# An order of the first units rewritten: a slice of weights fetched later, scores inside the preceding y, k scaled on GpSimd, the first product in two widths

## The chip, the cores and the metric

The kernel runs on one core of one Trainium2 chip. The metric is the device time of one execution in microseconds. All times below come from the profile of one execution of the kernel before, from its trace, or from the three timed runs.

## What is computed

Two stages follow each other. The first is a recurrent retention over 4 batches, 8 heads, 768 steps and a head size of 64; its output, turned to 3072 rows of 512, goes through a gated layer with the weights w_in (512 x 2048) and w_out (2048 x 512):

```python
for t in range(S):
    state = gamma[None, :, None, None] * state + np.einsum('bhd,bhe->bhde', k[:, :, t], v[:, :, t])
    y[:, :, t] = scale * np.einsum('bhd,bhde->bhe', q[:, :, t], state)
...
h = x @ w_in
g = h * (1.0 / (1.0 + np.exp(-h)))
return (g @ w_out)
```

The inputs q, k and v are float32, the weights are float64.

## The kernel before

**Units and products.** The sequence is cut into 6 chunks of 128 steps; a chunk of one batch is a unit, numbered chunk by chunk, so that units 0 to 3 are the four batches of chunk 0. When the four units of a chunk have been through the first stage, their output x (512 rows of 512) is multiplied by 16 slices of w_in, each of 128 columns. "Product (c, f)" is chunk c by slice f. The products are kept, after the gate, in DRAM (`g_dram`), and the second half of the kernel multiplies them by w_out. For accuracy x and the weights are each split in three parts, and a product is 12 matmuls of 512 columns: 8 into `ha`, 4 into `hb`.

**Steps of a unit.** `T(n)` (`stage_t`) transposes k and q on TensorE (L476, from unit 10 on in halves, L485), and ScalarE copies the results out (L477). `K(n)` (`scale_k`, L418) scales k in place. `SC(n)` makes the sums over k and v (`stage_s`, L504) and the scores (`stage_a`, L514). `A(n)` is called three times: the decay mask on VectorE (L522), the middle state (L528 on ScalarE in chunk 0, L530 on VectorE later) and the next state (L534). `Q(n)` (L423) scales q. `YA(n)` and `YB(n)` are the two halves of the unit's output y on TensorE (`stage_y`, L562); between them stands a fence, a one-element memset on GpSimd (L406) that waits for the first half. `X(n)`, called in turn, copies y out (L609) and splits it in three: L633 on ScalarE, then `lower` (L636) and `third` (L639) on VectorE. `KA(n)` scales k on ScalarE (L909).

**Weights.** `load_w(i)` fetches slice i with three transfers (one at L186 and two at L188, 512 KB in all) into one of two staging buffers. `W(i)`, called step by step, turns float64 into float32 (L205 and L212 on ScalarE, L208, L214, L218 and L224 on VectorE) and splits it (L121, L124, L127, L129). `CL(f)` takes a product out: a copy from `ha` on ScalarE (L744), the subtraction of `hb` on VectorE (L749), the gate on ScalarE (L754); `put_g` stores it (L760).

**Order.** The instructions of the first part, up to the line `early_order.close()`, stand on every engine in the order in which the code writes them. `T(10)`, the first step behind that part, meets q of unit 10. TensorE's instructions stand in written order all through. `fill` and `narrow` are matmuls of zeros that are put in where TensorE would pause; their numbers stand in tables (`FILL_T`, `FILL_Y` and so on), by unit. The transposed k and the two accumulators of a product take turns in three PSUM banks (`turn`), so that every third use meets the same bank.

**Transfers.** All go through SP's queue, in its order: k, q and v of unit 0, the first slice of w_in, units 1 to 3, the second slice, units 4 and 5, the third slice, units 6 and 7, the first stored product, and so on:

```python
for n in range(EARLY - 2):
    for name in "kqv":
        load(name, n)
    if n in (0, 3):
        load_w(n // 3)
```

`EARLY` is 8 and `FAR` is 14. q from unit 8 on has two buffers, k and v three.

Of the kernel before, what the change touches and what calls it, by code (L numbers as in the profile page):

```python
# [34 lines left out]
def kernel(  # L35
# [28 lines left out]
    nc = tc.nc  # L64
# [248 lines left out]
    def fill(out, n, start=True):  # L313

        cols = out.shape[-1] // 128
        for _ in range(n):
            nc.tensor.matmul(out, lhsT=zero, rhs=zero.unsqueeze(1).to_broadcast([128, cols, 128]),
                             start=start, stop=True, skip_group_check=True)

    def narrow(out, n):  # L320

        for _ in range(n):
            nc.tensor.matmul(out[:, :32], lhsT=zero, rhs=zero[:, :32], start=True, stop=True,
                             skip_group_check=True)

    for n in range(EARLY - 2):
        for name in "kqv":
            load(name, n)
        if n in (0, 3):
            load_w(n // 3)  # L330


    ident = const.tile([128, 128], FP32, tag="ident", name="ident")
# [58 lines left out]
    def banks(tag, name, n=2):  # L392
        return ps_u.tile([128, n, 512], FP32, tag=tag, name=name)
# [17 lines left out]
    def scale_k(n):  # L411
        if 0 <= n < len(units):
            t = kqv["k"][n]
            if units[n][0] == NC - 1:
                t = t[:D]
            g = gk[: t.shape[0], units[n][0], :].unsqueeze(2).to_broadcast([t.shape[0], H, D])
            engine = nc.gpsimd if 2 * B + 1 < n < FAR else nc.vector
            engine.tensor_tensor(out=t, in0=t, in1=g, op=ALU.mult)  # L418

    def scale_q(n):  # L420
# [29 lines left out]
        nc.scalar.copy(out=to[n].bitcast(U16).rearrange("p a (t w) -> p w a t", w=2),  # L450
                       in_=turned.pop((name, n)).rearrange("p (w a) t -> p w a t", w=2))

    FILL_T = {2: (3, 2), 3: (0, 1)}
    NARROW_T = {0: (8, 5)}
    FILL_Y = {0: 1, 3: 4}
    NARROW_Y = {0: 8}
    idle = []
    FILL_FENCE = {0: 2, 2: 2, 3: 2}
    FILL_P = {(0, 0): 1, (1, 0): 2}

    def stage_t(n):

# [28 lines left out]

    def score_tile(n):
        u = banks("s", f"sc_{n}")
        sc, sums = (u[:, :, ts(i, 4 * D)].rearrange("p o (a t) -> p o a t", a=HP)
                    for i in range(2))
        return sc, sums
# [46 lines left out]
    def stage_y(n):  # L543

        vs, amn, qtn = kqv["v"].pop(n), am.pop(n), qt.pop(n)
        states = steps_of.pop(n)
        bank = banks("y", f"y_{n}")
        fill(bank[:, 0], FILL_Y.get(n, 0))
        narrow(bank[:, 0], NARROW_Y.get(n, 0))
        yp = bank[:, :, : 4 * D].rearrange("p o (a t) -> p o a t", a=HP)  # L550
        lone = None
        if n == len(units) - 1:
            lone = banks("s", f"yl_{n}")[:, :, : 4 * D].rearrange("p o (a t) -> p o a t", a=HP)

        started, done, new = set(), [], []

        def product(a, o, j, lhsT, rhs, apart_now=False):
            e = j ^ (a % 2)
            to = lone if apart_now else yp
            o = o ^ 1 if apart_now else o  # L560
            key = apart_now, e, o
            i = nc.tensor.matmul(to[ts(e, D), o, a, :], lhsT=lhsT, rhs=rhs,  # L562
                                 start=key not in started, stop=True,
                                 skip_group_check=True).ins
            started.add(key)
            if new:
                fence(done[-1], i)
                new.clear()
            done.append(i)

        def scores():
            for a in range(HP):
                for o in range(2):
                    for j in range(2):
                        product(a, o, j, vs[ts(o, D), 2 * a + j, :], amn[ts(o, D), j, a, :])

        def states_with(part):

            if lone is None:
                new.extend([part] * part)  # L580
            for a in range(HP):
                for o in range(2):
                    j = o ^ part
                    if states[o] is not None:
                        product(a, o, j, states[o][ts(j, D), a, :], qtn[ts(j, D), a, ts(o, D)],
                                part == 1 and lone is not None)
            if part == 0:
                fill(bank[:, 0, 4 * D :], FILL_FENCE.get(n, 0), False)

        if lone is not None:  # L590
            alone[:] = [lone]
        return scores, states_with, yp
# [6 lines left out]
    def steps_y(n, yp):  # L599
        c, b = units[n]  # L600
        if b == 0:
            p, tag = (wpool, "wq") if c == LATE else (xpool, "xt")
            xt[c] = p.tile([128, 3, KIN, NT], FP32R, tag=tag, name=f"xt_{c}")
        raw = None
        if c < LATE:
            if n == 0:
                raws.append(wpool.tile([128, LATE * B, KIN, C], FP32, tag="wq", name="ys"))
            raw = raws[0][:, n]
            nc.scalar.copy(out=raw.rearrange("p a (o t) -> p o a t", o=2), in_=yp)  # L609
        elif c == LATE:  # L610
            raw = hpool.tile([128, KIN, C], FP32, tag="hs", name=f"ys_{n}")
            nc.scalar.copy(out=raw.rearrange("p a (o t) -> p o a t", o=2), in_=yp)
            nc.sync.dma_start(out=y_dram[b], in_=raw)
        elif alone:
            raw = hpool.tile([128, KIN, C], FP32, tag="hs", name=f"ys_{n}")
            to = raw.rearrange("p a (o t) -> p o a t", o=2)
            nc.scalar.copy(out=to, in_=yp)
            for o in range(2):
                for e in range(2):
                    x, z = (t[ts(e, D), i, e ^ o ^ 1 :: 2, :]  # L620
                            for t, i in ((to, o), (alone[0], 1 - o)))
                    nc.vector.tensor_tensor(out=x, in0=x, in1=z, op=ALU.add)
        yield from split_x(c, b, yp, raw)

    def split_x(c, b, y, raw):
        yield
        x = [xt[c][:, i, :, ts(b, C)] for i in range(3)]
        if raw is None:
            src = y
            xh, xl = (t.rearrange("p a (o t) -> p o a t", o=2) for t in x[:2])  # L630
        else:
            (xh, xl), src = x[:2], raw
        held[:] = [nc.scalar.activation(out=xh, in_=src, func=AF.Copy, scale=HALF).ins]  # L633

        def lower():
            nc.vector.tensor_tensor(out=xl, in0=src, in1=xh.bitcast(FP32), op=ALU.subtract)  # L636

        def third():
            nc.vector.scalar_tensor_tensor(out=x[2], in0=x[1].bitcast(FP32),  # L639
                                           scalar=-1.0 / EPS, in1=x[0].bitcast(FP32),  # L640
                                           op0=ALU.mult, op1=ALU.add)

        def rest():
            lower()
            third()

        if c > LATE or c == LATE and y is not None:
            behind_next.append(rest)
            return
        yield  # L650
        lower()
        yield
        third()
# [75 lines left out]
    def multiply(c, f):  # L729
        ha, hb = turn(f"ha_{c}_{f}"), turn(f"hb_{c}_{f}")  # L730
        fill(ha, FILL_P.get((c, f), 0))
        for i in range(3):
            for kk in range(KIN):
                nc.tensor.matmul(hb if i == 2 else ha, lhsT=w_sb[f][:, i, ts(kk, 128)],  # L734
                                 rhs=xt[c][:, i, kk, :], start=kk == 0 and i != 1,
                                 stop=kk == KIN - 1 and i != 0)
        return ha, hb

    def close_in(*of):
        list(close_steps(*of))  # L740
# [91 lines left out]
    def YA(n):  # L832
        ys[n] = stage_y(n)
        ys[n][0]()
        ys[n][1](0)

    def YB(n):
        ys[n][1](1)
        ysteps[n] = steps_y(n, ys[n][2])

    def X(n):
        next(ysteps[n], None)
# [3 lines left out]
    def W(i, times=1):  # L846
        if i not in slices:
            slices[i] = early_slice(i)
        for _ in range(times):
            next(slices[i], None)  # L850
# [11 lines left out]
    T(0), K(0)  # L862
    nc.scalar.activation(out=token, in_=lgc[:1, :1], func=AF.Silu)
    SC(0), A(0), Q(0), A(0), A(0)
    W(0), W(0), W(0), W(0), W(0)
    YA(0), YB(0), X(0)
    T(1), K(1)
    W(0)
    load_w(2)
    W(0)  # L870
    X(0), X(0)
    SC(1), A(1)
    W(0)
    A(1)
    Q(1), A(1)
    T(2), K(2)
    W(0), X(0)
    W(0), W(0)
    YA(1), SC(2)
    A(2)  # L880
    YB(1), X(1)
    A(2), Q(2), A(2)
    X(1)
    T(3), K(3)
    X(1), X(1)
    YA(2), YB(2), X(2)
    SC(3), A(3), A(3), Q(3), A(3)
    X(2), W(1), W(1)
    X(2), X(2)
    YA(3), YB(3), X(3), X(3)  # L890
    W(1), W(1)
    T(4)
    X(3), X(3)
    K(4)
    W(1), W(1)
    loads(EARLY - 2), loads(EARLY - 1)
    closing = {}

# [10 lines left out]
            nc.scalar.activation(out=t[:, h, :], in_=t[:, h, :], func=AF.Copy,  # L909
                                 scale=gk[:, units[n][0], h : h + 1])  # L910

    P(0)
    next_chunk()
    SC(4)
    CL(0), CL(0), CL(0)
# [239 lines left out]
```

## Time and profile before

| What | us |
|---|---|
| median of three runs | 613.96 |
| the three runs | 614.32, 613.96, 612.52 |
| profiled execution | 614.34 |
| its span, first to last instruction | 612.6 |
| TensorE matmul busy | 600.9 (98%) |
| VectorE busy | 397.1 (65%) |
| ScalarE busy | 324.5 (53%) |
| GpSimd busy | 32.9 (5%) |

PE is TensorE's matmul row, PEld its weight loads, DVE VectorE, ACT ScalarE, POOL GpSimd, SPq the queue of SyncE that issues the transfers. A busy TensorE isn't TensorE at its peak, since matmuls overlap. The granted clock of TensorE is 1.00 over the span. "Slices" on the page are 40 equal parts of the span, 15.3 us each, and each digit is a share in tenths.

### The profile page before, as it was taken

What the parts mean: (1) busy time and instruction counts of PE and PEld (TensorE: products, weight loads), DVE (VectorE), ACT (ScalarE), POOL (GpSimd) and SP (SyncE); (2) the same over time, 40 slices, a digit from 0 to 9 for tenths busy, and PEclk for the clock granted to TensorE, in tenths of its full rate; (3) what the DMA queues carried; (4) which work ended last, traced back from release to release, by engine and by line L of the source; (5) the groups of instructions that cost most, each with busy time, mean ns of one, the idle gap of its engine ahead of it and who ended that gap; (6) DMA issues with size and microseconds to landing.
All of it is one profiled execution on the core that took longest, in us unless ns stands there. A gap on an engine that the chain in (4) does not pass through costs nothing.

```text
span 612.6 us, 13713 instructions
## 1 busy us (share of the span) xinstructions
PE 600.9 (98%) x5509; PEld 495.9 (81%) x5509; DVE 397.1 (65%) x672; ACT 324.5 (53%) x598; POOL 32.9 (5%) x89
## 2 busy tenths in 40 slices
PE   8898999999999999999999999999999999999997
PEld 6686788888888888888888888888888888888886
DVE  4797898678886676766689774635545463645631
ACT  7688678678676667676698632212221322313211
POOL 3000020100021111210000000000000000000000
PEclk9999999999999999999999999999999999999999
DMA  9999976586799699998777542623524433433301
GB/s 195 209 199 231 258 214 203 160 254 188 258 231 233 154 263 263 258 291 255 248 249 267 169 138 69 206 69 106 169 72 136 137 110 97 152 123 99 107 1 69
DMA packets 144336, 108.90 MB, mean 178 GB/s; under 512 B 101137, under 2 KB 109585, under 8 KB 144273
## 3 DMA queue, kind: packets, MB, share of 16 engines
q1 hardware_dynamic: 144272, 108.03, 62.3%
q8 instruction: 43, 0.70, 0.5%
q14 instruction: 21, 0.16, 0.1%
HBM read 66.06 MB, written 36.70 MB: 168 GB/s over the span
## 4 chain that ended last, share of the span: by engine, by line
PE 92%; DMA 3%; SPq 2%; DVE 2%; issue 1%; ACT 0%; DVEq 0%
PE ha L734 28%; PE o L1088 21%; PE oa L1088 14%; PE hb L734 14%; PE ob L1088 7%; PE y L562 3%; DMA qf<-in_q_dram 2%; PE sc L504 1%; SPq L166 1%; PE sc L514 1%; DMA kqv<-in_v_dram 1%; SPq L188 1%; PE o L1102 0%; PE oa L1102 0%; PE kp L485 0%
## 5 line engine op out<-in xcount | busy, mean ns | idle before, releaser
L734 PE MATMUL ha<-xt,wi 128*128 128x512 f32 x768 | 193.0, 393 | 0.0
L734 PEld LDWEIGHTS ha<-xt,wi 128*128 128x128 f32 x768 | 142.4, 188 | 30.5 <-DVE xt L636 0.2
L1088 PE MATMUL o<-wo,gs 128*128 128x512 f32 x564 | 143.1, 389 | 0.0
L805 ACT ACTIVATE gs<-gr 128x512 fp32r<-128x512 f32 x96 | 53.2, 621 | 139.0 <-issue 138.0
L1088 PEld LDWEIGHTS o<-wo,gs 128*128 128x128 f32 x564 | 105.9, 188 | 22.0
L807 DVE TENSOR_TENSOR gs<-gr,gs 128x512 fp32r<-128x512 f32 x96 | 62.1, 684 | 94.2 <-ACT gs L805 94.2
L1088 PE MATMUL oa<-wo,gs 128*128 128x512 f32 x376 | 115.7, 389 | 0.0
L749 DVE TENSOR_TENSOR g<-g,hb 128x512 f32<-128x512 f32 x96 | 65.7, 684 | 57.6 <-ACT g L744 42.6
L734 PE MATMUL hb<-xt,wi 128*128 128x512 f32 x384 | 102.7, 389 | 0.0
L734 PEld LDWEIGHTS hb<-xt,wi 128*128 128x128 f32 x384 | 72.1, 188 | 15.1
L1088 PEld LDWEIGHTS oa<-wo,gs 128*128 128x128 f32 x376 | 70.5, 188 | 14.6
L754 ACT ACTIVATE g<-g 128x512 f32<-128x512 f32 x96 | 60.3, 629 | 37.7 <-DVE g L749 37.6
L1088 PE MATMUL ob<-wo,gs 128*128 128x512 f32 x188 | 73.1, 389 | 0.0
L744 ACT ACTIVATE g<-ha 128x512 f32<-128x512 f32 x96 | 56.7, 591 | 28.6 <-PE ha L734 19.8
L808 DVE SCALAR_TENSOR_TENSOR gs<-gs 128x512 fp32r<-128x512 f32 x96 | 62.0, 683 | 0.1
L1088 PEld LDWEIGHTS ob<-wo,gs 128*128 128x128 f32 x188 | 35.3, 188 | 7.4
L205 ACT ACTIVATE ca<-wf 128x512 f32<-128x512 f32 x32 | 21.6, 675 | 6.6 <-DVE cs L218 4.0
L522 DVE TENSOR_TENSOR am<-sc,decay 128x512 f32<-128x512 f32 x24 | 16.5, 687 | 11.4 <-PE sc L514 11.4
L1112 ACT ACTIVATE o<-o 128x512 f32<-128x512 f32 x10 | 6.0, 598 | 33.4 <-PE o L1088 33.0
L218 DVE SCALAR_TENSOR_TENSOR cs<-ca,cs 128x512 uint32<-128x512 uint32 x32 | 22.7, 710 | 0.9
L639 DVE SCALAR_TENSOR_TENSOR xt<-xt 128x512 fp32r<-128x512 f32 x28 | 19.9, 715 | 0.7
L562 PE MATMUL y<-qt,mid 64*64 64x64 f32 x376 | 19.4, 220 | 0.4 <-issue 0.4
(122 smaller groups left out, 562.2 us busy)
## 6 DMA issues: line engine op xcount, KB each, us to landing
gd<-g SPq DMA_DIRECT2D x96, 256.0 KB, 3.7
gr<-gd SPq DMA_DIRECT2D x96, 256.0 KB, 2.7
wf<-in_moe_w_out_dram SPq DMA_DIRECT2D x16, 512.0 KB, 4.7
out_dram<-o SPq DMA_DIRECT2D x23, 256.0 KB, 2.1
wf<-in_moe_w_in_dram SPq DMA_DIRECT2D x16, 256.0 KB, 4.6
wf<-in_moe_w_in_dram SPq DMA_DIRECT2D x32, 128.0 KB, 4.1
kf<-in_k_dram SPq DMA_DIRECT2D x16, 256.0 KB, 4.1
qf<-in_q_dram SPq DMA_DIRECT2D x16, 256.0 KB, 4.1
```

The source lines that it names most:

```text
L205: top = nc.scalar.activation(out=a.bitcast(FP32), in_=hi.bitcast(FP32), func=AF.Abs, scale=2.0 ** -3).ins
L218: nc.vector.scalar_tensor_tensor(out=s, in0=a, scalar=3, in1=s, op0=ALU.logical_shift_left, op1=ALU.bitwise_xor)
L562: i = nc.tensor.matmul(to[ts(e, D), o, a, :], lhsT=lhsT, rhs=rhs, start=key not in started, stop=True, skip_group_check=True).ins
L639: nc.vector.scalar_tensor_tensor(out=x[2], in0=x[1].bitcast(FP32), scalar=-1.0 / EPS, in1=x[0].bitcast(FP32), op0=ALU.mult, op1=ALU.add)
L734: nc.tensor.matmul(hb if i == 2 else ha, lhsT=w_sb[f][:, i, ts(kk, 128)], rhs=xt[c][:, i, kk, :], start=kk == 0 and i != 1, stop=kk == KIN ...
L744: copied[:] = [nc.scalar.activation(out=hs, in_=ha, func=AF.Copy, scale=ONE_E).ins]
L749: taken_out[:] = [nc.vector.tensor_tensor(out=hs, in0=hs, in1=hb, op=ALU.subtract).ins]
L754: nc.scalar.activation(out=hs, in_=hs, func=AF.Silu)
L805: nc.scalar.activation(out=t[:, 0, :], in_=g, func=AF.Copy, scale=HALF)
L807: nc.vector.tensor_tensor(out=t[:, 1, :], in0=g, in1=high, op=ALU.subtract)
L808: nc.vector.scalar_tensor_tensor(out=t[:, 2, :], in0=t[:, 1, :].bitcast(FP32), scalar=-1.0 / EPS, in1=high, op0=ALU.mult, op1=ALU.add)
L1088: nc.tensor.matmul(o, lhsT=g, rhs=wo[f][:, i, :], start=f == 0 and i != 1, stop=f == NF - 1 and i != 0)
```

## The change

The first slice of w_in is fetched behind k, q and v of unit 2 instead of unit 0. `K(n)` runs on GpSimd for units 1 to 13 where it is called (before: units 10 to 13), and `lower` does so for units 0 to 2. The order is written anew: the transposes of unit n+1 come ahead of y of unit n, and the scores of units 1 to 3 between the two halves of the preceding y; the conversion of the first slice comes behind unit 2's y. The tables of zero matmuls differ, with two new ones (`FILL_S`, `NARROW_FENCE`). Unit 3 is split from PSUM without the copy L609. The first product is made in pieces by `multiply_first`: its first four matmuls in two widths, 384 columns (units 0 to 2) and 128 (unit 3), ahead of `T(4)`, the other eight behind it.

```diff
-        if n in (0, 3):
-            load_w(n // 3)
+        if n in (2, 3):
+            load_w(n - 2)
...
-            engine = nc.gpsimd if 2 * B + 1 < n < FAR else nc.vector
+            engine = nc.gpsimd if 0 < n < FAR else nc.vector
...
-    FILL_T = {2: (3, 2), 3: (0, 1)}
+    FILL_T = {1: (0, 2), 2: (1, 1), 3: (0, 2)}
     NARROW_T = {0: (8, 5)}
-    FILL_Y = {0: 1, 3: 4}
-    NARROW_Y = {0: 8}
+    FILL_Y, NARROW_Y, NARROW_FENCE = {3: 3}, {}, {}
+    FILL_FENCE = {2: 2, 3: 2}
+    FILL_P = {(1, 0): 2}
+    FILL_S = {3: (1, 8)}
     idle = []
-    FILL_FENCE = {0: 2, 2: 2, 3: 2}
-    FILL_P = {(0, 0): 1, (1, 0): 2}
...
         u = banks("s", f"sc_{n}")
+        fill(u[:, 0], FILL_S.get(n, (0, 0))[0])
+        narrow(u[:, 0], FILL_S.get(n, (0, 0))[1])
...
-        if c < LATE:
+        if n == B - 1:
+            pass
+        elif c < LATE:
...
-            nc.vector.tensor_tensor(out=xl, in0=src, in1=xh.bitcast(FP32), op=ALU.subtract)
+            engine = nc.gpsimd if c == 0 and b < B - 1 else nc.vector
+            engine.tensor_tensor(out=xl, in0=src, in1=xh.bitcast(FP32), op=ALU.subtract)
...
+    def multiply_first():
+
+        ha, hb = turn("ha_0_0"), turn("hb_0_0")
+        for cols in (ds(0, (B - 1) * C), ds((B - 1) * C, C)):
+            for kk in range(KIN):
+                nc.tensor.matmul(ha[:, cols], lhsT=w_sb[0][:, 0, ts(kk, 128)],
+                                 rhs=xt[0][:, 0, kk, cols],
+                                 start=kk == 0 and cols.start == 0, stop=False,
+                                 skip_group_check=True)
+            yield
+        for i in range(1, 3):
+            for kk in range(KIN):
+                nc.tensor.matmul(hb if i == 2 else ha, lhsT=w_sb[0][:, i, ts(kk, 128)],
+                                 rhs=xt[0][:, i, kk, :], start=kk == 0 and i == 2,
+                                 stop=kk == KIN - 1, skip_group_check=True)
+        yield ha, hb
...
     SC(0), A(0), Q(0), A(0), A(0)
-    W(0), W(0), W(0), W(0), W(0)
-    YA(0), YB(0), X(0)
     T(1), K(1)
-    W(0)
+    YA(0), SC(1), YB(0)
+    A(1), X(0), A(1), Q(1), A(1)
+    T(2), K(2)
+    X(0)
+    YA(1), SC(2), YB(1)
+    X(0)
+    A(2), X(1), A(2), Q(2), A(2), X(1)
+    X(0)
+    YA(2), YB(2)
+    X(1)
+    W(0), X(2)
+    W(0), W(0), W(0)
+    T(3), K(3)
+    X(1)
+    X(2), X(2)
+    W(0), W(0), W(0)
     load_w(2)
     W(0)
-    X(0), X(0)
-    SC(1), A(1)
-    W(0)
-    A(1)
-    Q(1), A(1)
-    T(2), K(2)
-    W(0), X(0)
+    SC(3)
+    A(3), Q(3), A(3)
     W(0), W(0)
-    YA(1), SC(2)
-    A(2)
-    YB(1), X(1)
-    A(2), Q(2), A(2)
-    X(1)
-    T(3), K(3)
-    X(1), X(1)
-    YA(2), YB(2), X(2)
-    SC(3), A(3), A(3), Q(3), A(3)
-    X(2), W(1), W(1)
-    X(2), X(2)
-    YA(3), YB(3), X(3), X(3)
-    W(1), W(1)
+    X(2)
+    first = multiply_first()
+    YA(3), YB(3)
+    next(first)
+    X(3), X(3)
+    next(first)
+    X(3), W(0)
     T(4)
-    X(3), X(3)
+    X(3), A(3)
     K(4)
-    W(1), W(1)
+    W(1), W(1), W(1), W(1), W(1), W(1)
     loads(EARLY - 2), loads(EARLY - 1)
...
-    P(0)
+    closing[0] = close_steps(0, 0, *next(first))
     next_chunk()
```

More of the change, by code (lines that the diff above doesn't have):

```diff
@@ L318, in fill, with narrow @@
                              start=start, stop=True, skip_group_check=True)
-    def narrow(out, n):
+    def narrow(out, n, start=True):
         for _ in range(n):
-            nc.tensor.matmul(out[:, :32], lhsT=zero, rhs=zero[:, :32], start=True, stop=True,
+            nc.tensor.matmul(out[:, :32], lhsT=zero, rhs=zero[:, :32], start=start, stop=True,
                              skip_group_check=True)
@@ L588, in states_with @@
                 fill(bank[:, 0, 4 * D :], FILL_FENCE.get(n, 0), False)
+                narrow(bank[:, 0, 4 * D :], NARROW_FENCE.get(n, 0), False)
         if lone is not None:
```

## The prediction

> **What bounds the kernel now.** I read the page first, then the chain of waits over the first 80 us, TensorE's waits behind that, the timeline where the chain changes hands, and the transfers. Two lines of the page, the DMA share in 40 slices and the chain's shares by engine:
>
> ```profile
> DMA  9999976586799699998777542623524433433301
> ...
> PE 92%; DMA 3%; SPq 2%; DVE 2%; issue 1%; ACT 0%; DVEq 0%
> ```
>
> TensorE owns the chain, but not from the beginning: for five slices of 15.3 us the transfer engines are 90% busy or more. Pieces of the chain over 0 to 80 us (start, length, what):
>
> ```profile
> 11.45 6.06 DMA kqv<-in_v_dram
> ...
> 30.76 0.69 DVE g L749
> ...
> 46.03 0.59 SPq L166
> 46.62 0.04 issue
> 46.67 11.82 DMA qf<-in_q_dram x2
> 58.49 0.04 issue
> 58.54 0.27 PE kp L485
> ```
>
> So the first 58.5 us belong to transfers and SP's issues, with a VectorE stretch from 30.7 to 44; then q of unit 10 lands at 58.49. From there every later piece is TensorE. The waits of TensorE between 58 and 613 us (total, times, longest) are one row:
>
> ```profile
> PE kp L485 <- DMA qf<-in_q_dram: 1.1, 1, 1.1
> ```
>
> After it TensorE never waits again. The time is therefore when unit 10's q lands, plus 554 us of TensorE work which the diff leaves alone. The timeline at three places where TensorE meets q:
>
> ```profile
> 27.06 0.60 PE L476 MATMUL qp<-ident,kqv 128*128 128x128 f32 x4 [0.43 <-issue]
> ...
> 52.73 0.63 PE L476 MATMUL qp<-ident,qf 128*128 128x128 f32 x4 [0.26 <-DMA qf<-in_q_dram]
> ...
> 58.54 0.27 PE L485 MATMUL kp<-ident,qf 64*128 64x64 f32 x1 [1.09 <-DMA qf<-in_q_dram]
> ```
>
> They are units 4, 9 and 10 (the first names no transfer, but the half before it, of k, is done and only q is missing). Unit 6 is nearly such a place: q lands at 36.16, its transposes start at 36.43. The transfers up to 60 us:
>
> ```profile
> DMA packets 38513, 12.49 MB, mean 208 GB/s; under 512 B 35556, under 2 KB 38116, under 8 KB 38500
> ...
> q8 instruction: 10, 0.16, 1.4%
> ```
>
> SP issues almost without a pause until 58 us, and its issues are long (0.6 to 2.9 us) because what is in flight is bounded: three or four transfers after SP has finished an issue. The ten instruction fetches take 1.4% of 16 engines over 60 us, 0.014 x 16 x 60 / 10 = 1.34 us each; some 2 us after several of them the rate of a 1.5 us slice falls from about 250 to 121 to 139 GB/s, so I take a fetch to hold up the stream by about its length.
>
> **The change part by part.** The sum is made against the profiled execution: span 612.6, time 614.34, thus 1.7 outside; the median of the runs is 613.96, 0.4 lower.
>
> *The first slice of w_in behind unit 2.* Three transfers, 512 KB, change place with k, q, v of units 1 and 2; from the twelfth place on SP's list is as it was. By the same bytes at the same places, v of unit 1 lands at about 10.7 instead of 12.3, v of unit 2 at 13.7 instead of 17.5, the slice at 17.5 instead of 9.8. Unit 3 (20.0), the second slice (23.4), q of unit 4 (27.06) and all that follow, q of unit 10 included, keep their times. The slice is then split: L205 0.66, L214 0.43, L218 0.69, L224 0.68, L121 0.62 give its high part about 3.3 after landing, near 21, its last part near 23; it is first needed after unit 3's y, near 23.5. Covered; if it weren't, q of unit 4 at 27.06 still comes later. The third slice reuses the first one's staging buffer, free when L205, L208 and L212 have read it, at about 20; SP reaches that issue at 27.3. No queue moves.
>
> *Scores inside the preceding y* (units 1 to 3). The same matmuls in another order: transposes of unit n+1 ahead of y of n, scores between its halves. It closes the 1.1 us that TensorE waits for v of unit 2 before 17.73 and starts unit 3's scores at about 20.3 instead of 22.3. All ends at the transposes of unit 4, whose q comes at 27.06 either way: worth nothing by itself. Zero matmuls: 41 before, 37 after, in idle time; with the four more matmuls of the split product the count of TensorE's instructions up to unit 10 is equal, and so the number of fetches.
>
> *First product in two widths.* Four matmuls of 384 columns and four of 128 (4 x 0.227 = 0.9 us of columns) run ahead of unit 4's transposes, in the pause before 27.06. Behind them stay 8 x 0.227 = 1.8 instead of a zero matmul and 12: the product ends at about 29.5 instead of 30.66, 1.1 earlier. Its two accumulators are now taken ahead of unit 4's transposes, so unit 5's k transposes get the bank of ha and wait for the copy L767: I put them at 31.1, against 31.67. Unit 6 then stands ready about 0.2 to 0.5 earlier and waits for q at 36.16. Gain kept: 0.3 at most, and unit 9 takes it away again.
>
> *Scaling of k on GpSimd* (units 1 to 5, 7, 8) and three lower parts of x (L642). On VectorE it holds the engine 0.60 (0.68 less overlap), on GpSimd L418 takes 1.04 to 1.32. VectorE is the bound in 30.7 to 44; units 4, 5, 7 and 8 lie there or behind, so up to 4 x 0.60 = 2.4 us come off it. Against that, VectorE and GpSimd rows of the same moment:
>
> ```profile
> 68.85 1.32 POOL L418 TENSOR_TENSOR kf<-kf,gk 128x512 f32<-128x512 f32 x1
> ...
> 69.19 1.53 DVE L636 TENSOR_TENSOR xt<-ys,xt 128x512 fp32r<-128x512 f32 x1
> ```
>
> L636 takes 0.68 elsewhere: beside the GpSimd scaling it loses 0.84. Per scaling the VectorE chain goes by -0.60 (nothing meets it) to +0.24 (0.84 - 0.60); four make -2.4 to +1.0. I take about -0.5, since VectorE is nearly full there and most scalings will meet something, though not every operation is hit (L749 at 77.29, into which the next scaling runs, stays at 0.68; it takes one input from PSUM). [...] On GpSimd's own queue the fences (L406) of the y stand behind the scalings, but each scaling needs only k and transposes done earlier on TensorE, so it is finished before the fence is due.
>
> All of this meets two walls: q of unit 9 at 52.60, where TensorE now arrives 0.26 early, and q of unit 10 at 58.49, where it arrives 1.09 early. An earlier VectorE is wasted; one later by 1.0 goes into the 1.09. **Sum: 0**, with -0.3 to 0 for what fits between the walls. In the runs' terms 613.8.
>
> **The rivals.** *Faster, the transfers themselves come earlier.* For it: the stream isn't at a fixed rate, it dips after fetches, and their moments shift as TensorE runs ahead. Against: bytes, count and order from the twelfth on are the same. If one dip of 1.34 falls out ahead of unit 9, TensorE's 1.09 at unit 10 goes, and the VectorE relief of units 7 and 8 (2 x 0.60 = 1.2) becomes visible: -2.3, 611.7.
>
> *Slower, GpSimd holds up the chain.* Place: units 4, 5, 7, 8. If VectorE is there only waiting on TensorE, the relief is worth nothing and each scaling costs the full 0.84: 3.4, of which 1.09 is idle time now: +2.3, 616.2. It decides from a delay of 1.1 at unit 10's k. For it: the L636 row. Against: L749 isn't hit, and the chain shows VectorE as bound.
>
> *Slower, the stream comes later*: two dips more ahead of unit 10, 2 x 1.34 = +2.7, 616.6. Against: same instruction count.
>
> *The moves don't bind at all* (TensorE doesn't arrive earlier anywhere): gives 613.9, and is one with the forecast in time.
>
> **How the numbers follow.** No change 0.59, transfers earlier 0.23 (the dips are the least understood thing in the sum, and here TensorE runs ahead of where it was), GpSimd 0.12, transfers later 0.06. A measurement of this kernel tells about 0.3% (1.8 us) from no change; the three runs lie 1.8 apart. Faster 0.23, same 0.59, slower 0.18. The range takes in the first two rivals: 611.5 to 616.2.
>
> **What would show it.** Right: q of unit 10 again lands within 1 us of 58.5 and is again TensorE's only wait behind 58 us, 1 to 2 long; the first product ends near 29.5; unit 2's scores no longer wait for v; L418 stands under GpSimd at 1.0 to 1.3. Wrong: unit 10's q lands before 57 or after 60, or TensorE comes to it without waiting, or it waits again later.

## The result, and the profile after

The changed kernel takes 617.24 us in the median (614.89 to 618.62, seven runs) where the kernel before takes 614.24 beside it: 1.0045 times as long, 95% interval 1.0025 to 1.0066. Forecast were 613.8 and a range up to 616.2. The profiled execution took 617.38 us, its span is 615.6, 3.0 more than before; TensorE is busy for 600.9 us as before. The two lines of the page that were shown of before:

```profile
DMA  8998786585699799999777542523524433432301
...
PE 93%; DVE 2%; ACT 2%; DMA 1%; issue 1%; SPq 1%; POOL 0%; DVEq 0%; ACTq 0%; POOLq 0%
```

The share of DMA in the chain has fallen from 3% to 1%, and VectorE, ScalarE and "issue" stand there instead. Pieces of the chain over 0 to 62 us (start, length, what):

```profile
3.70 6.10 DMA kqv<-in_q_dram
...
18.58 1.41 DVE cs L208
19.99 1.19 DVE ca L214
...
22.42 1.76 DVE cs L224
24.18 0.61 DVE am L524
...
48.78 1.52 issue
...
51.31 1.30 POOL kf L418
...
53.94 1.05 issue
...
60.02 0.20 PE kp L485
```

No transfer stands in it behind 9.8 us. q of unit 10 lands at 55.75, 2.7 us earlier than before, and TensorE turns to unit 10 only at 59.95, with the transposes of k, 3.0 later than the first trace of before did (56.98); those of q follow at 60.25, 1.7 later than before (58.54). The waits of TensorE between 58 and 613 us are one row again, but another one:

```profile
PE hb L740 <- ACT g L767: 0.4, 1, 0.4
```

The start of the loss is seen where VectorE and GpSimd stand side by side, in the timeline of 16 to 25 us, first VectorE (its first and last line are the masks of units 2 and 3), then GpSimd:

```profile
16.42 0.69 DVE L524 TENSOR_TENSOR am<-sc,decay 128x512 f32<-128x512 f32 x1 [2.52 <-PE sc L516]
...
18.49 1.50 DVE L208 TENSOR_SCALAR cs<-wf 128x512 uint32<-128x512 uint32 x1
19.91 1.26 DVE L214 TENSOR_SCALAR ca<-ca 128x512 f32<-128x512 f32 x1
...
22.42 1.76 DVE L224 CUSTOM_DVE_ANT_0 cs<-cs,cw 128x1024 uint16<-128x1024 uint16 x1
24.10 0.68 DVE L524 TENSOR_TENSOR am<-sc,decay 128x512 f32<-128x512 f32 x1
```

```profile
18.39 1.32 POOL L642 TENSOR_TENSOR xt<-ys,xt 128x512 fp32r<-128x512 f32 x1
19.67 1.22 POOL L418 TENSOR_TENSOR kqv<-kqv,gk 128x512 f32<-128x512 f32 x1
22.23 1.39 POOL L642 TENSOR_TENSOR xt<-ys,xt 128x512 fp32r<-128x512 f32 x1 [1.35 <-ACT xt L638]
```

Alone L208, L214 and L224 take 0.42, 0.42 and 0.69 us. Here each ends 0.28, 0.28 and 0.56 us behind the end of the GpSimd operation beside it: it was held until about then and lost 1.08, 0.84 and 1.07, in all 3.0 us. VectorE works without a pause from 17.9 to 25.7 us, and unit 3's mask (L524), for which TensorE waits 1.0 us at 23.8, comes behind all three.

### The profile page after: what moved, and what is told of

It reads as the page before. It is cut to its first block, busy times and chain, and to the rows that moved or that the text cites. A ratio compares the mean times of both kernels' runs of the same rounds, so it can differ in the third digit from the quotient of the medians.

```text
span 615.6 us, 13720 instructions
## 1 busy us (share of the span) xinstructions
PE 600.9 (98%) x5509; PEld 495.2 (80%) x5509; DVE 396.3 (64%) x662; ACT 323.9 (53%) x597; POOL 47.8 (8%) x99
## 4 chain that ended last, share of the span: by engine, by line
PE 93%; DVE 2%; ACT 2%; DMA 1%; issue 1%; SPq 1%; POOL 0%; DVEq 0%; ACTq 0%; POOLq 0%
PE ha L740 28%; PE o L1113 21%; PE oa L1113 14%; PE hb L740 14%; PE ob L1113 7%; PE y L564 4%; PE sc L506 2%; PE sc L516 2%; DMA kqv<-in_q_dram 1%; PE kp L476 1%; SPq L166 1%; DMA gd<-g 0%; PE qp L476 0%; PE o L1127 0%; ACT gq L379 0%
## 5 line engine op out<-in xcount | busy, mean ns | idle before, releaser
L740 PEld LDWEIGHTS ha<-xt,wi 128*128 128x128 f32 x760 | 140.7, 188 | 31.1 <-DVE g L772 0.7
L767 ACT ACTIVATE g<-ha 128x512 f32<-128x512 f32 x96 | 56.6, 590 | 24.6 <-PE ha L740 11.8
L524 DVE TENSOR_TENSOR am<-sc,decay 128x512 f32<-128x512 f32 x24 | 16.5, 687 | 13.6 <-PE sc L516 13.5
L645 DVE SCALAR_TENSOR_TENSOR xt<-xt 128x512 fp32r<-128x512 f32 x28 | 22.9, 824 | 0.6
```

Source lines behind the costliest of these rows:

```text
L767: copied[:] = [nc.scalar.activation(out=hs, in_=ha, func=AF.Copy, scale=ONE_E).ins]
```

## The experiments

Three theories were set against each other: *GpSimd* (its operations hold up VectorE's where VectorE sets the end), *order* (the conversion of the first slice between units 2 and 3 is late, on whatever engine) and *instruction supply* (TensorE's two stretches of "issue" above). The ratios, all to the kernel before run beside it, and two readings of each trace: by how much VectorE operations beside a GpSimd one took longer than alone, ahead of 26 us and from 26 to 62 us.

| Kernel | Ratio (95%) | Median us | Excess to 26 us | 26 to 62 us |
|---|---|---|---|---|
| the change | 1.0045 (1.0025 to 1.0066) | 617.24 | 2.99 | 1.77 |
| e0, the change again | 1.0076 (1.0049 to 1.0104) | 619.09 | 2.99 | 0.52 |
| e13, the change again | 1.0066 (1.0035 to 1.0096) | 618.53 | 3.00 | 1.33 |
| e1, lower parts on VectorE | 1.0033 (1.0015 to 1.0052) | 616.61 | 0.72 | 1.85 |
| e2, scaling on VectorE | 1.0042 (1.0019 to 1.0066) | 616.49 | 2.15 | 0 |
| e3, both on VectorE | 1.0009 (0.9980 to 1.0037) | 614.53 | 0 | 0 |
| e12, as e3 | 0.9998 (0.9971 to 1.0026) | 614.40 | 0 | 0 |
| e4, old order, both on GpSimd | 1.0013 (0.9991 to 1.0036) | 615.41 | 1.26 | 2.46 |
| e7, GpSimd early only | 1.0063 (1.0040 to 1.0086) | 618.25 | 3.00 | 0 |
| e8, GpSimd late only | 1.0042 (1.0019 to 1.0065) | 616.21 | 0 | 2.64 |
| e10, the change, more zero matmuls | 1.0032 (1.0013 to 1.0051) | 617.18 | 3.00 | 1.22 |
| e5, e3 with more zero matmuls | 1.0004 (0.9981 to 1.0028) | 615.29 | 0 | 0 |
| e6, e3 shifted | 1.0031 (1.0010 to 1.0053) | 616.98 | 0 | 0.62 |
| e9, e3 shifted further | 1.0059 (1.0039 to 1.0079) | 618.19 | 0 | 0.62 |
| e11, e3 and unused GpSimd work | 1.0127 (1.0087 to 1.0167) | 621.43 | not summed | not summed |

The 0.62 of e6 and e9, and 0.77 of e8, are a meeting with the scaling of unit 10, which runs on GpSimd in every version and meets an operation of VectorE ahead of 62 us in these three alone.

**The change again, and its two GpSimd edits taken back, one and both.** e0 is the change as it is. e1:

```diff
-            engine = nc.gpsimd if c == 0 and b < B - 1 else nc.vector
-            engine.tensor_tensor(out=xl, in0=src, in1=xh.bitcast(FP32), op=ALU.subtract)
+            nc.vector.tensor_tensor(out=xl, in0=src, in1=xh.bitcast(FP32), op=ALU.subtract)
```

e2 (e3 has both edits):

```diff
-            engine = nc.gpsimd if 0 < n < FAR else nc.vector
+            engine = nc.gpsimd if 2 * B + 1 < n < FAR else nc.vector
```

> The changed kernel unaltered, as the yardstick of this set: 617.2 us, 1.0045 of the kernel before. What the second trace is for: TensorE came to unit 10's q transposes 1.71 us late, and slipped another 1.3 us between 166 and 205 us, where ScalarE waits for a store to free a buffer. If the later slip is this one execution's, the second trace shows a shift that stays near 1.7 us behind 60 us and a span near 614.3. If it follows from the early part, it comes again, at the same place and near 1.3 us.

> The changed kernel with the three lower parts of x (L642) back on VectorE; the scalings of k stay on GpSimd. Theory GpSimd: in the changed kernel three VectorE operations of the x chain of units 2 and 3 beside a GpSimd operation took 1.50, 1.26 and 1.76 instead of 0.42, 0.42 and 0.68, in all 3.0 us; two of them (1.08 + 1.08 = 2.2 us) were beside L642. Without these the chain up to unit 4's k is 2.2 shorter less three subtractions of 0.7 on VectorE, of which one stands ahead of unit 3's mask: 1.0 to 2.0 us come back, 615.2 to 616.2. Theory order (the conversion of the first slice between units 2 and 3 delays the chain, whatever the engine): no change or up to 0.7 us slower, 617.2 to 617.9.

> The changed kernel with the scalings of k of units 1 to 5, 7 and 8 back on VectorE; the lower parts stay on GpSimd. Theory GpSimd: the scaling beside L214 (0.84 us), the one at 28.7 beside L208 (0.52), the one at 51.3 beside L645 (0.6), for which TensorE also waits 0.3, go; VectorE takes 0.60 for each scaling instead. With the chain bound by VectorE from 17.9 to 31 this is nearly even there, and a gain of 0.3 to 0.9 in unit 8: 616.3 to 616.9. Theory order: 617.2, or slower by up to 2 x 0.60 for scalings that the relief had saved.

> The changed kernel with both on VectorE: of the change the place of the slice, the scores inside y and the split first product are left. Theory GpSimd: TensorE is again bound by the transfers, whose last one (q of unit 10) landed at 55.75 in the changed kernel, 2.7 us earlier than before; the time falls below that of the kernel before or equals it, 612 to 614.2. Theory order: VectorE has all of its work again, the chain of conversion, first product and x is late with it, 617 to 619. Theory instruction supply (two stretches of 1.5 and 1.05 us, at 48.8 and 53.9 us, in which TensorE waits for nothing that the trace shows, each behind a fetch of instructions): these stretches stay, and at least 2 us of the 3 us by which unit 10's k was late stay with them, 616 to 617.

With both on VectorE the loss is gone: e3 and its repeat e12 are the kernel before within their intervals, 1.0009 and 0.9998. So the rest of the change (place of the slice, scores inside y, split product) is worth nothing that these runs can tell, and *order* by itself falls as the cause. Each half alone still loses 0.3 to 0.4%; together that is 0.75%, and the whole took 0.45 to 0.76%. Three numbers were missed: e0 took 619.09 instead of 617.2; e1, at 616.61, gave back 2.5 us against e0 beside it, but lies above 615.2 to 616.2; and e3's 614.53 is just above 612 to 614.2. VectorE of e12 in the stretch that was shown of the change:

```profile
17.16 0.69 DVE L524 TENSOR_TENSOR am<-sc,decay 128x512 f32<-128x512 f32 x1 [1.27 <-PE sc L516]
...
19.84 0.42 DVE L208 TENSOR_SCALAR cs<-wf 128x512 uint32<-128x512 uint32 x1
20.17 0.42 DVE L214 TENSOR_SCALAR ca<-ca 128x512 f32<-128x512 f32 x1
...
23.05 0.68 DVE L224 CUSTOM_DVE_ANT_0 cs<-cs,cw 128x1024 uint16<-128x1024 uint16 x1
23.65 0.68 DVE L524 TENSOR_TENSOR am<-sc,decay 128x512 f32<-128x512 f32 x1
```

From unit 2's mask (17.16 here, 16.42 in the change) to unit 3's it is 23.65 - 17.16 = 6.49 us, with three more operations on VectorE, and 24.10 - 16.42 = 7.68 in the change; e0 and e13 give 7.67 and 7.68 as well. The difference of 1.19 is what the collisions leave: 3.0 less 3 x 0.60 of relief.

In e0 the expected 1.3 us later slip came again (1.84 at 150 us, 3.39 at 205); in e13 it did not. What it is stays open (below).

**The kernel before again, the old order with GpSimd, more zero matmuls, and fewer instructions.** b1 is the kernel before. e4 is the kernel before with the two GpSimd lines of the change. e5 and e6 start from e3:

```diff
-    FILL_Y, NARROW_Y, NARROW_FENCE = {3: 3}, {}, {}
+    FILL_Y, NARROW_Y, NARROW_FENCE = {3: 3, 4: 3}, {}, {}
...
-    FILL_S = {3: (1, 8)}
+    FILL_S = {3: (1, 8), 8: (2, 0)}
```

```diff
-    narrow(idle[0], 39)
-    fill(idle[0], 2)
-    narrow(idle[0], 39)
+    fill(idle[0], 7)
```

> The kernel before, unaltered, for a second trace: how steady are its transfers and its TensorE. In its first trace q of unit 10 landed at 58.49, TensorE's granted clock was 1.000, and it lost nothing at the boundary of 256 instructions at which every changed kernel so far lost 1.05 to 2.32 us (before its instruction 2498, at 51 to 57 us). Theory instruction supply as a property of the changed order: less than 0.3 us lost there again. Theory that the first trace of before was a lucky one: 1 us or more is lost there in this one too.

> The kernel before with only the two GpSimd edits (scaling of k of units 1 to 5, 7, 8 and the three lower parts of x), in the old order, with the slice ahead and the first product whole. Theory GpSimd: the collisions do not need the new order; with both edits the changed kernel lost 0.0067 against the same kernel without them, so 1.003 to 1.008 of the kernel before, 616.4 to 619.5 us. Theory of the two together (GpSimd hurts only where the conversion of the slice stands between units 2 and 3, so that VectorE has no slack): 0.999 to 1.002, 613.9 to 615.8.

> The version with both on VectorE, with three zero matmuls more ahead of unit 4's y and two ahead of unit 8's scores, where TensorE stood idle for 0.83 and 0.47 us. Theory clock: in the traces of the variants TensorE's granted clock falls to 0.50 for 3.4 us after a stretch of that length in which it was about half busy or less (busy shares 0.32 to 0.54), which costs up to 1.7 us; the zero matmuls lift the stretch at 32 to 36 us from 0.54 to about 0.73, so fewer of the runs show a lowered clock and the median falls by 0.5 to 1.0 against the version without them. Theory that idle time costs only itself: no change, or slower by up to 0.3 where a zero matmul stands ahead of work that is ready.

> The version with both on VectorE, with 78 narrow and 2 wide zero matmuls of the start replaced by 7 wide ones of about the same length: TensorE has 146 instructions less ahead of everything else. Theory instruction supply: TensorE goes on fetching in blocks of 256, so the lost stretches stay at its own instructions 706, 962, 2242 and 2498 and move in the program by 146 instructions; the scores of unit 9 ahead of which 1.81 us were lost come without a wait, and a stretch of 1 to 2 us is lost 146 instructions later, near the transposes of unit 10 or behind them, where wide matmuls follow; the time changes by -1.5 to +0.5. Theory of another cause (a bank, a semaphore, the release of a buffer that the trace does not show): the stretch stays ahead of the scores of unit 9, of the same length.

b1 took 619.10 us in its one run, and its trace overturns what the prediction took from the first one. The timeline of TensorE in b1:

```profile
53.81 0.22 PE L562 MATMUL y<-qt,state 64*64 64x64 f32 x1
56.42 0.27 PE L562 MATMUL y<-qt,state 64*64 64x64 f32 x1 [2.40 <-issue]
...
62.65 0.27 PE L485 MATMUL kp<-ident,kf 64*128 64x64 f32 x1
```

The kernel before loses 2.40 us at the same boundary, before instruction 2498 (of TensorE's own count, with its weight loads and its semaphore instructions), and its unit 10 starts at 62.65 although q had landed at 57.45. The loss there is thus no property of the new order; the first trace of before had been spared it (0.13). This holds against *instruction supply* as the cause of the change's loss, not against the effect itself.

e4 is at 1.0013, and at most at 1.0036, although operations of the conversion collide here too. L224 in the first trace of before, then in e4:

```profile
12.28 0.68 DVE L224 CUSTOM_DVE_ANT_0 cs<-cs,cw 128x1024 uint16<-128x1024 uint16 x1
```

```profile
12.11 1.31 DVE L224 CUSTOM_DVE_ANT_0 cs<-cs,cw 128x1024 uint16<-128x1024 uint16 x1
```

In e4 L124, at 15.62, takes 1.33 as well, where 0.68 is its length alone. But in the old order little of this reaches TensorE: unit 3's mask starts at 22.83 instead of 23.55, unit 4's k transposes at 26.31 instead of 25.98, its q transposes at 26.80 instead of 27.06. The theory of the two together fits; the theory that the collisions alone suffice, with its 1.003 to 1.008, does not fit the 1.0013, though the interval touches its lower end. Nor is the cost shown to be nothing: e4's runs had a mean granted clock of 0.9990 against 0.9981 of the kernel before beside it, worth some 0.5 us in its favour. A collision costs where VectorE sets the end, which the new order brought about.

e5: one of 12 runs had a mean granted clock below 0.998, where e3 had four, but the median did not fall; no gain. e6: the boundaries moved with the count, as instruction supply says. Nothing is lost in its trace at 50 to 60 us, unit 10's q comes 1.10 earlier than in the first trace of before, and the loss turns up elsewhere, before its own instruction 5314 (5314 = 194 + 20 x 256):

```profile
185.79 0.23 PE L564 MATMUL y<-qt,state 64*64 64x64 f32 x2
187.87 0.21 PE L564 MATMUL y<-qt,mid 64*64 64x64 f32 x1 [1.85 <-issue]
```

The time rose instead of falling. What the runs of e6 lost beside this is not known. Other zero matmuls, with the boundaries shifted by them, thus cost about as much here as the change does (e9 below, 1.0059, too). That does not touch the comparison of the change with e3 and e12, e7 and e8, since TensorE has the same instructions in the same order in all of these.

**GpSimd at one place only, a further shift, and zero matmuls ahead of unit 3's y.** e7 and e8 are the change with these lines:

```diff
-            engine = nc.gpsimd if 0 < n < FAR else nc.vector
+            engine = nc.gpsimd if 0 < n < B or 2 * B + 1 < n < FAR else nc.vector
```

```diff
-            engine = nc.gpsimd if 0 < n < FAR else nc.vector
+            engine = nc.gpsimd if B <= n < FAR else nc.vector
...
-            engine = nc.gpsimd if c == 0 and b < B - 1 else nc.vector
-            engine.tensor_tensor(out=xl, in0=src, in1=xh.bitcast(FP32), op=ALU.subtract)
+            nc.vector.tensor_tensor(out=xl, in0=src, in1=xh.bitcast(FP32), op=ALU.subtract)
```

e9 is e6 with one wide zero matmul in place of each group of narrow ones in unit 0, e10 the change with `FILL_Y = {3: 8}`.

> The changed kernel with GpSimd kept for the early operations only: the scalings of k of units 1 to 3 and the three lower parts of x. Units 4, 5, 7 and 8 are scaled on VectorE. So far: the changed kernel 1.0045 and 1.0076 of the kernel before, the same with both on VectorE 1.0009, and the old order with both on GpSimd 1.0013. Theory early collisions (in the new order VectorE bounds the chain from 17.5 to 26 us, where the slice's conversion stands between units 2 and 3, and each collision there is paid): nearly all of the loss stays, 1.003 to 1.007, 616.4 to 618.8. Theory of the prediction's rival (units 4, 5, 7 and 8 are the place): the loss goes, 0.999 to 1.002, 613.9 to 615.7.

> The counterpart: GpSimd kept for the scalings of units 4, 5, 7 and 8 only, all that stands ahead of them on VectorE. Theory early collisions: as the version with both on VectorE, 0.999 to 1.002, 613.9 to 615.7. Theory of the prediction's rival: 1.003 to 1.007, 616.4 to 618.8. If both this and its counterpart lose about 0.3% each, the places add up, and neither theory holds alone.

> The shifted version (both on VectorE, 146 instructions of TensorE less at the start) with 13 narrow zero matmuls of unit 0 replaced by two wide ones, another 22 instructions less. In the trace of the shifted version nothing was lost at the boundaries of 256 instructions up to 60 us, and unit 10's q transposes came 1.1 us earlier than before; but 1.85 us were lost at 186 us, at instruction 5314, which is a boundary too. Counting the same trace with boundaries 22 instructions later, the shortest block between two boundaries from 55 us on takes 4.7 us (4.08 at 51 us), against 3.7 where the 1.85 were lost. Theory instruction supply: the loss at 186 us goes and no other of over 0.5 us takes its place behind 60 us; 1.5 to 2 us less than the shifted version, 0.999 to 1.001 of the kernel before. Theory of another cause at 186 us: a stretch of over 1 us without work stays there, and the time stays at 1.003.

> The changed kernel with five zero matmuls more (1.1 us) ahead of unit 3's y, where TensorE stood idle 1.0 to 2.0 us for unit 3's mask. In the second trace of the changed kernel the 3.4 us ahead of that y were 0.37 to 0.42 busy, and the granted clock fell to 0.50 from 26.8 to 30.2 us; all eight of its runs showed such a fall, against 4 of 12 with both on VectorE. Theory clock: a good part of what GpSimd costs is the clock, 1.7 us for each fall; with the zero matmuls 1 to 3 us come back against 1.0045 to 1.0076, thus 1.001 to 1.004, and fewer runs show a lowered clock. Theory that the collisions cost only their own length: no change, 1.0045 to 1.0076.

The early operations alone cost 1.0063, as much as all of them: this is the main place. But the late ones alone cost 1.0042 against 0.9998 and 1.0009 without any, so the place of the prediction's rival counts too, and neither theory holds alone. e9 went the other way than expected: its trace loses nothing at 186 us, but 1.40 at 194.71, at instruction 5570, again a boundary, after a block of 256 that takes 5.2 us by itself (189.47 to 194.71). A block of 4.7 was thought to be safe; it isn't.

e10 came out as expected for the clock, at 1.0032: TensorE's idle stretch ahead of unit 3's y is 0.89 instead of 1.97 us in e0, and 5 of 12 runs show a lowered clock instead of all 8 of e0. Its interval overlaps that of the change, so this alone would not show it.

**Collision or late result.** In e11, GpSimd does the work of the ten operations once more behind VectorE, in parts of 128 columns, into a tile that nobody reads:

```diff
+            if 0 < n <= 2 * B + 1:
+                for h in range(0, H, 2):
+                    nc.gpsimd.tensor_tensor(out=lag.rearrange("p (h d) -> p h d", h=2), in0=t[:, h : h + 2, :],
+                                            in1=g[:, h : h + 2, :], op=ALU.mult)
...
+            if c == 0 and b < B - 1:
+                for k in range(KIN):
+                    nc.gpsimd.tensor_tensor(out=lag, in0=xh.bitcast(FP32)[:, k], in1=xl.bitcast(FP32)[:, k], op=ALU.subtract)
```

> The version with both on VectorE, and behind each of the ten operations GpSimd does the same amount once more (two parts behind each scaling, four behind each lower part) into a tile that nobody reads. VectorE has no relief, and nobody waits for GpSimd's result. Theory collision: VectorE operations beside these take up to twice their time or more (1.2 to 1.8 us instead of 0.4 to 0.7), and the time rises by 0.003 to 0.008 against the version without them: 616.4 to 619.5 us. Theory late result: TensorE and VectorE wait for a scaling or a lower part that GpSimd ends 0.4 to 0.9 later than VectorE would; with nobody waiting, no change against the version without them, within 0.002.

> The version with both on VectorE once more, as the lower end for the run with unused GpSimd work: 0.998 to 1.004 of the kernel before by its first measurement.

> The changed kernel once more, as the upper end on the same chip: 1.003 to 1.010 of the kernel before, and above the version with both on VectorE by 0.002 to 0.007.

(The first insert makes four parts behind each scaling, not two as the expectation says: H is 8.) Nobody waits for this work, and yet it costs 1.0127 against 0.9998, more than the 0.003 to 0.008 of the expectation. Its VectorE in the same stretch:

```profile
23.05 0.94 DVE L651 SCALAR_TENSOR_TENSOR xt<-xt 128x512 fp32r<-128x512 f32 x1
23.92 0.88 DVE L645 TENSOR_TENSOR xt<-ys,xt 128x512 fp32r<-128x512 f32 x1
24.72 0.88 DVE L224 CUSTOM_DVE_ANT_0 cs<-cs,cw 128x1024 uint16<-128x1024 uint16 x1
25.53 0.68 DVE L528 TENSOR_TENSOR am<-sc,decay 128x512 f32<-128x512 f32 x1
```

All but the last stand beside GpSimd and take 0.2 to 0.26 us more than alone; from unit 2's mask (17.08) to unit 3's it is 8.45 instead of 6.49 us. So the collision costs by itself, without a wait for GpSimd's result. That the late result costs nothing in the change is not shown by this: its chain has one such piece, unit 8's k at 51.31.

**What makes 1.2 us into 3.6.** Beside each other on one chip, the mean of e13 is 618.35 us and that of e12 614.78. Of these 3.6 us, 1.2 are the collisions of the early stretch. The rest is seen in e13's windows (columns: TensorE busy, its weight loads, VectorE, ScalarE, GpSimd, granted clock, DMA share, GB/s):

```profile
23.40:26.10 2.70, 0.73 (x37) 0.64 (x38) 2.70 (x5) 0.98 (x2) 0.26 (x1) 1.00 1.05 201
26.10:33.00 6.90, 6.80 (x43) 5.80 (x37) 3.41 (x7) 2.94 (x6) 1.13 (x2) 0.51 1.04 225
33.00:36.00 3.00, 3.00 (x76) 2.44 (x75) 1.85 (x4) 2.25 (x8) 0.00 (x0) 1.00 1.20 214
```

TensorE waits for unit 3's mask, and from 26.1 on its granted clock is 0.51 for 6.9 us, just when the first product runs:

```profile
25.46 0.69 PE L564 MATMUL y<-am,kqv 64*64 64x64 f32 x32 [1.97 <-DVE am L524]
...
27.72 1.65 PE L750 MATMUL ha<-xt,wi 128*128 128x384 f32 x4
```

Four matmuls of 384 columns take 1.65 us here, where four of 384 and four of 128 took 1.43 in the first trace of the change, whose clock stayed at 1.000. e0 and e7 show the same fall, of 3.4 and 6.8 us, at the same place and behind the same 1.97 us; e12 keeps 1.00 there with 0.49 us of idle time. Over the runs the mean granted clock is 0.9951 in e13 (10 of 12 runs below 0.998) and 0.9987 in e12 (3 of 12). Worked out, (0.9987 - 0.9951) x 615 = 2.2 us at full clock: with the 1.2 that is 3.4 of the 3.6 measured. This sum is an estimate. A straight line of time against mean clock, through the 47 runs of these two and of the kernel before beside them, agrees with it: it gives 0.67 us for each 0.001 of clock and leaves 1.2 us between e13 and e12 at equal clock, with a standard error of 0.6. The two traces alone would not have shown it: their spans are 615.0 and 614.7, because e12's execution had a fall of its own, of 3.4 us from 54.6 on. Nor does the clock explain every execution: the first trace of the change lost its 3.0 us at a clock of 1.000, 1.7 of them up to unit 10 and 1.4 between 150 and 210 us. That the idle stretch brings the fall is supported by these traces and by e10, which keeps the collisions whole (3.00) and the clock at 0.9982 in the mean: its mean is 616.92 us, 2.0 above the kernel before beside it, where e13's is 3.2 above.

## Why the prediction was wrong

*The slice and the scores.* Worth nothing, as forecast: v of unit 1 landed at 10.80 (put at 10.7), v of unit 2 at 13.72 (13.7), and without GpSimd the new order takes the time of the kernel before. Wrong in two points. What follows the twelfth transfer did not keep its times: unit 3's v landed at 21.77 (put at 20.0), q of unit 4 at 25.36 (27.06). And the slice's conversion was called covered, "near 21" and "near 23"; L224 ended at 24.18, and unit 3's mask stands behind it.

*First product.* Its last matmul was put at 29.5; it ended at 30.94, later than the 30.66 of before, since unit 3's y and with it the whole product waited for the mask. Unit 5's k transposes were put at 31.1 and came at 32.59, behind the copy L767.

*Scaling on GpSimd* is the step that failed. It weighed four scalings, of units 4, 5, 7 and 8, against the 0.84 of one row, and took -0.5. The three lower parts and the scalings of units 1 to 3 were named and got no price, though they run beside the conversion of the slice, which the same change had moved there. Priced by the shown pair of rows, three collisions at 0.84 less three operations at 0.60 would have been +0.7, where 1.2 was measured; the size of one was 0.52 to 1.09 in the traces of the change. Nor is it only operations like L636 in those rows, which reads two tiles, that are held up: L208 and L214, with one tile read and 0.42 us alone, lost 1.08 and 0.84 us in the change and ended 0.28 us behind the GpSimd operation beside them. Why, the traces don't show.

*The rival "GpSimd holds up the chain"* (0.12) had the right mechanism and nearly the right time, 616.2. Its place, units 4, 5, 7 and 8, was the smaller one by e7 and e8, and the 1.09 us of idle time that it set against its price weren't there.

*The two walls.* The sum of 0 rested on q of unit 9 and 10 landing late, read from one trace. q of unit 10 landed at 55.75 in the change and at 57.45 in b1, and TensorE waited for it in neither. The kernel before is therefore not "554 us of TensorE work behind a landing": over these traces and the first one of before, 58.49, the landing moves by 2.7 us, and what TensorE loses before its instruction 2498 by 2.3 (0.13 and 2.40 in the two traces of before). By the prediction's own test (q before 57, or TensorE comes to it without waiting) the step was wrong. The first place, unit 4 at 27.06, was no wall of q's either as far as the trace shows: the 0.43 us of "issue" stand before instruction 1218 = 194 + 4 x 256, 1.53 us behind the end of an instruction fetch (24.54 to 25.53), as at the other boundaries below, and no row gives q's landing; those of k and v are at 24.36 and 27.37.

*Idle time of TensorE* was priced at its own length. It can also cost clock: the falls in the traces of e0 and e12 lasted 3.4 us at 0.50, which is 1.7 us of full clock, those of e7 and e13 6.8 and 6.9 us.

*Open.* TensorE slips by another 0.6 to 2.0 us between 150 and 205 us in six of the traces with scalings on GpSimd (the change, e0, e1, e4, e7, e8), where ScalarE waits for a store to free a buffer; not in e10 and e13, nor in those with all on VectorE, save for the instruction boundaries of e6 and e9. No run tests it. It is also not settled why the late operations alone (e8) cost 0.4%: their trace has unit 10's q 0.73 earlier than the first trace of before, and loses only behind 150 us. No version beat the kernel before.

## What to carry to other kernels

Before work moves to GpSimd, list what VectorE does at the same moments, in the new order, and put a price on each meeting: the three ahead of 26 us in the change lost 0.84 to 1.08 us each and ended 0.28 to 0.56 us behind the GpSimd operation. Whether VectorE has slack there decides what reaches the end: the same move cost nothing clear of the noise in the old order (e4, 1.0013) and 0.5 to 0.8% in the new one. An idle stretch of TensorE near 2 us is worth guarding even where its own length seems cheap, because the clock can fall behind it: in e0, e7 and e13 it was at 0.50 for 3.4 to 6.9 us behind 1.97 us. One trace gives one draw of the transfers: a second trace of the unchanged kernel (b1) has q of unit 10 at 57.45 instead of 58.49, and TensorE's start on unit 10 at 62.65 instead of 56.98.

## What the runs showed of the hardware

TensorE's instructions came in blocks of 256. The traces of before and of the change each have 43 instruction fetches of 16 KB (0.9 to 1.9 us) for TensorE's 11,080 and 11,083 instructions, which behind the first 194 make 42.5 blocks of 256. Over the traces, stretches of "issue" of more than 0.4 and up to 2.4 us come before instructions 706, 962, 1218, 1986, 2242, 2498, 5314 and 5570 of its own count, all 194 and a multiple of 256, wherever the program has got to by then. Next to those of the traces of before and of the change, the fetch (1.0 to 1.4 us) begins 1.5 to 2.6 us after TensorE has crossed the boundary before, and the first instruction of the new block runs 1.5 us after its end: in the change, fetch 52.03 to 53.47, first instruction 54.99. Before instructions 706, 2242 and 2498 of the change these three times together are 4.2, 5.2 and 4.7 us, the block was through after 3.7, 3.7 and 3.6, and 0.5, 1.5 and 1.1 were lost. That TensorE had run out of instructions there is inferred from the fetch beside each stretch; no row names what it waited for. The longest stretch is the 2.40 us of b1.

The granted clock fell to 0.50 without a full pause. In e1, e2 and e3 it fell, around 53 to 58 us, behind 3.4 us in which TensorE was 0.49, 0.32 and 0.47 busy, no idle stretch being longer than 2.32 us. Not each such stretch brings a fall: the 3.4 us ahead of 18.3 in e7 and of 19.0 in e5 were 0.42 busy, and the clock stayed at 1.00 behind them. What decides it, these traces don't show.
